# Reading attention heads back from a DRAM scratch: whole 128-row tiles against 20-row transfers over two groups

## Chip, cores, metric

One core of one Trainium2 chip. The metric is the device time of one execution in microseconds (us), lower is better.

## The reference

Two layers, each made of an attention with a compressive memory and a feed-forward block, on 2048 tokens of width 640, with 32 heads of only 20 features. The attention runs over four segments of 512 tokens per layer, one after the other.

```python
B, S, D, H = (1, 2048, 640, 32); N = 4; L = S // N          # Dh = 20
for s in range(N):
    logits = einsum('bhqd,bhkd->bhqk', qs, ks) * scale + mask
    p = softmax(logits); a_dot = einsum('bhqk,bhkd->bhqd', p, vs)
    a_mem = (phi(qs) @ M) / (phi(qs) @ z + 1e-06)
    outs.append(g * a_mem + (1.0 - g) * a_dot)
    M = M + phi(ks).T @ vs;  z = z + phi(ks).sum()
# ... [cut: layer norms before, output projection, residual, then x + relu(LN(x) @ w1) @ w2; all twice]
```

## The kernel before

Instructions are laid out by a list scheduler that runs while the program is built: it has a cost for each operation and fixes the order on every engine.

Queries and keys leave the projections as five chunks of 128 feature rows, without regard to heads (128 is no multiple of 20). The score matmuls of this kernel read the 20 rows of each head at partitions 0, 32, 64 and 96. So each chunk is *spilled* to a DRAM scratch, and each group of four heads is *read back* from there into a `pad` tile. All these transfers, and the transposing transfers, are issued by one in-order queue, that of the sync engine (SP; in the trace it issues all 40 spills, 64 read-backs and 54 transposes).

```python
NPAD = 10
pad = sb("pad", [128, NPAD, 2, L])
scr = nc.dram_tensor("scr", [2, D + 12, 2 * L], dt.bfloat16, kind="Internal").ap()

def spill(a, s):                                   # 5 chunks of a segment
    for c in range(FC):
        # ... [cut: wait for the evacuated chunk]
        tk = yield dma("sp", scr_sem[s % 2][c], 400000, lambda e, c=c: e.dma_start(
            scr[s % 2, 128 * c:128 * c + 128, :], stg[:, c].rearrange("p n t -> p (n t)")), ...)

def fill(a, s):                                    # 8 groups of a segment: the read-backs
    for g in range(G):
        # ... [cut: take a buffer sl, wait for the one or two chunks that hold the rows]
        row = scr[s % 2, 80 * g:80 * g + 1, :]
        tk = yield dma("sp", pad_sem[id(sl)], 400000, lambda e, sl=sl, row=row: e.dma_start(
            sl.ap.rearrange("p n t -> p (n t)"),
            bass.AP(tensor=row.tensor, offset=row.offset,
                    ap=[[DH * 2 * L, 4], [2 * L, 32], [1, 2 * L]])), w + sl.tks, issue=550.0)
```

The source of a read-back has three dimensions, written as [step, count]: 4 heads, 32 rows, 1024 elements. Of every 32 rows 12 are never used, because they belong to the next head; they only fill the partitions up to the next multiple of 32. Two other transfers: `xnT<-xn_tok` transposes a normalized segment so that it can be projected, and `phk<-phs` transposes the key features for the memory update.

The softmax here doesn't subtract the row's maximum and nothing guards it: scores larger than these inputs give would overflow.

Of the kernel before, what the change touches and what calls it, by code (L numbers as in the profile page):

```python
# [5 lines left out]
dt = mybir.dt  # L6
# [4 lines left out]
D = 640  # L11
H = 32
DH = 20
NSEG = 4
L = T // NSEG
DFF = 1728
TT = T // 128
FC = D // 128
G = H // 4
# [5 lines left out]
NFULL = DFF // 128  # L25
# [13 lines left out]
class Prog:  # L39
# [44 lines left out]
    def dma(self, e, fn, sem):  # L84
        self.pos[e] += 1
        self.dcnt[id(sem)] = self.dcnt.get(id(sem), 0) + 16
        tk = (sem, self.dcnt[id(sem)])
        self.ops[e].append(("op", fn, sem, 16))
        self.info[(id(sem), tk[1])] = ("dma%d" % id(sem), tk[1], dict(self.K[e]))
        return tk  # L90
# [217 lines left out]
def bass_interleave_layers__memory_aug_infini_attn__dense_activation_relu__prompt_kernel(  # L308
    nc, A_x, A_wq, A_wk, A_wv, A_wo, A_beta, B_x, B_w1, B_w2, out,
):  # L310
    with contextlib.ExitStack() as es:
        sb = lambda name, shape, dtype=dt.bfloat16: es.enter_context(nc.sbuf_tensor(name, shape, dtype))
        sem_ = lambda name: es.enter_context(nc.semaphore(name))
        P = Prog({e: sem_("clk_" + e) for e in ["act", "dve", "pool", "pe"]})
        S = Sched(P)


        NPAD, NXT, NXN, NPT = 10, 2, 2, 2
        wq_r = sb("wq_r", [128, FC, D])
        wk_r = sb("wk_r", [128, FC, D])  # L320
        wv_r = sb("wv_r", [128, FC, D])
# [14 lines left out]
        xn_tok = sb("xn_tok", [128, NXN, 2 * D])  # L336
        stg = sb("stg", [128, FC, 2, L])
        phs = sb("phs", [128, FC * L])
        pad = sb("pad", [128, NPAD, 2, L])
        rtmp = sb("rtmp", [128, 3, L])  # L340
        phk = sb("phk", [128, FC, NJ, 128])
        v_aug = sb("v_aug", [128, 2, NJ, H, DH + 1])
# [19 lines left out]
        STG = [[Slot(stg[:, c, n], "stg") for c in range(FC)] for n in range(2)]  # L362
        PAD = [Slot(pad[:, k], "pad") for k in range(NPAD)]
        pad_sem = {id(s): sem_("pad%d" % k) for k, s in enumerate(PAD)}
        scr = nc.dram_tensor("scr", [2, D + 12, 2 * L], dt.bfloat16, kind="Internal").ap()
        scr_sem = [[sem_("scr%d_%d" % (n, c)) for c in range(FC)] for n in range(2)]
        RT = [Slot(rtmp[:, k], "rt") for k in range(3)]
        PHK = Slot(phk, "phk")
# [8 lines left out]
        OT = [Slot(oT[:, 2 * FC * k:2 * FC * k + 2 * FC], "oT") for k in range(2)]  # L377
        ot_sem = {id(s): sem_("ot%d" % k) for k, s in enumerate(OT)}
        phk_sem = sem_("phk")
        z_sem = sem_("z")  # L380
        HT = Slot(hT, "hT")


# [47 lines left out]
        def consts():  # L431
            tb = yield dma("act", sem_("d_beta"), 16384, lambda e: e.dma_start(
                beta_bc[:], bass.AP(tensor=A_beta.tensor, offset=A_beta.offset, ap=[[0, 128], [1, H]])))
            t2 = yield pool(400, lambda e: e.memset(
                v_aug[:].rearrange("p b j h e -> p (b j h) e")[:, :, DH:DH + 1], 1.0))
            for b in range(2):
                VA[b].tks = [t2]
            za = yield dve(320, 1, lambda e: e.memset(w1_r[:, :, DFF:DFFP], 0.0))
            zb = yield dve(640, 1, lambda e: e.memset(w2_r[DFF - NFULL * 128:128, NFULL, :], 0.0))
            S.set("z1", tks=[za, zb])  # L440
            zr = DFF - NFULL * 128
            for n in range(2):
                tz = yield dma("act", z_sem, 24576, lambda e, n=n: e.dma_start(
                    scr[n, D:D + 12, :].rearrange("r (k t) -> (r k) t", k=2), w2_r[zr:zr + 24, NFULL, 0:512]), [zb])
            S.set("z2", tks=[tz])
            yield Need("stg", 0, 0, 0)
            te = yield act(32, lambda e: e.activation(gt[:, 0, :], beta_bc[:], ACT.Exp), [tb], psum=False)
            ta = yield dve(32, 1, lambda e: e.tensor_scalar(gt[:, 1, :], gt[:, 0, :], 1.0, None, ALU.add), [te])
            tr = yield dve(256, 1, lambda e: e.reciprocal(gt[:, 1, :], gt[:, 1, :]), [ta])
            tg = yield dve(32, 1, lambda e: e.tensor_tensor(gt[:, 2, :], gt[:, 0, :], gt[:, 1, :], ALU.mult), [tr])  # L450
            to = yield dve(128, 1, lambda e: e.tensor_copy(
                omg[:].rearrange("p g i hh o -> p g i (hh o)"),
                gt[:, 1, :].rearrange("p (g hh) -> p g hh", g=G)[:, :, None, :].to_broadcast([128, G, NJ, 4])), [tr])
            S.set("omg", tks=[to])
            tm = None
            for c in range(FC):
                h0, h1 = CH_H0[c], CH_H1[c]
                mc = maskg[:, CH_OFF[c]:CH_OFF[c + 1]].rearrange("p (h e) -> p h e", e=DH + 1)
                t3 = yield dve(21, 1, lambda e, mc=mc: e.memset(mc[:, :, DH:DH + 1], 1.0))
                t4 = yield dve(147, 1, lambda e, mc=mc, h0=h0, h1=h1: e.tensor_copy(  # L460
                    mc[:, :, 0:DH], gt[:, 2, h0:h1][:, :, None].to_broadcast([128, h1 - h0, DH])), [tg])
                t5 = yield pool(400, lambda e, mc=mc, n=h1 - h0, base=128 * c - DH * h0: e.affine_select(
                    out=mc, in_=mc, compare_op=ALU.is_ge, fill=0.0, base=base,
                    pattern=[[-DH, n], [0, DH + 1]], channel_multiplier=1), [t3, t4])
                tm = yield pool(400, lambda e, mc=mc, n=h1 - h0, base=DH - 1 + DH * h0 - 128 * c: e.affine_select(
                    out=mc, in_=mc, compare_op=ALU.is_ge, fill=0.0, base=base,
                    pattern=[[DH, n], [0, DH + 1]], channel_multiplier=-1), [t5])
            S.set("maskg", tks=[tm])
# [125 lines left out]
        def spill(a, s):  # L594
            for c in range(FC):
                ev = yield Need("stg", a, s, c)
                before = S.events.get(("filled", a, s - 2) if s > 1 else ("filled", a - 1, s + 2), [])
                tk = yield dma("sp", scr_sem[s % 2][c], 400000, lambda e, c=c: e.dma_start(
                    scr[s % 2, 128 * c:128 * c + 128, :], stg[:, c].rearrange("p n t -> p (n t)")),
                    ev + before, issue=350.0)  # L600
                S.set("packed", a, s, c, tks=[tk])

        def fill(a, s):
            got = []
            for g in range(G):
                sl = yield Acq(PAD)
                w = yield Need("z2")
                w = list(w)
                for c in range(80 * g // 128, min(FC - 1, (80 * g + 91) // 128) + 1):
                    t = yield Need("packed", a, s, c)  # L610
                    w += t
                row = scr[s % 2, 80 * g:80 * g + 1, :]
                tk = yield dma("sp", pad_sem[id(sl)], 400000, lambda e, sl=sl, row=row: e.dma_start(
                    sl.ap.rearrange("p n t -> p (n t)"),
                    bass.AP(tensor=row.tensor, offset=row.offset,
                            ap=[[DH * 2 * L, 4], [2 * L, 32], [1, 2 * L]])), w + sl.tks, issue=550.0)
                S.set("pad", a, s, g, tks=[sl, tk])
                got.append(tk)
            S.set("filled", a, s, tks=got)

# [111 lines left out]
        def scores(n):  # L732
            a, r = divmod(n, NSEG * G)
            s, g = divmod(r, G)
            pt = yield Acq(PTS)
            pd = yield Need("pad", a, s, g)
            sl, pd = pd[0], pd[1:]
            mk = []
            for u, js in enumerate(ROUNDS):
                yield Acq([X])  # L740
                yield Acq([Y])
                fns = []
                for z, j in enumerate(js):
                    N = L - 128 * j
                    o = 0 if z == 0 else 512 - N
                    for hh in range(4):
                        fns.append((lambda e, j=j, hh=hh, N=N, o=o: e.matmul(  # L747
                            ps[:, hh, o:o + N], sl.ap[32 * hh:32 * hh + DH, 0, 128 * j:128 * j + 128],
                            sl.ap[32 * hh:32 * hh + DH, 1, 128 * j:L]), z == len(js) - 1 and hh in (1, 3)))
                w = PT_W[u]  # L750
                t0, t1 = yield pe(200.0 + w / 2.4, fns, pd + X.tks + Y.tks)
                ex = []
                for k, (bkp, tk) in enumerate(((X, t0), (Y, t1))):
                    tx = yield act(2 * w, lambda e, k=k, bkp=bkp, u=u, w=w: e.activation(  # L754
                        pt.ap[:, 2 * k:2 * k + 2, PT_AT[u]:PT_AT[u] + w], bkp.ap[:, :, 0:w], ACT.Exp, scale=SCALE),
                        [tk] + pt.tks)
                    bkp.release(tx)
                    ex.append(tx)
                for j in js:
                    reg = pt.ap[:, :, PT_OFF[j]:PT_OFF[j] + 128]  # L760
                    tm = yield pool(600.0, lambda e, reg=reg: e.affine_select(  # L761
                        out=reg, in_=reg, pattern=[[0, 4], [1, 128]], compare_op=ALU.is_ge, fill=0.0, base=0,
                        channel_multiplier=-1), ex)
                    mk.append(tm)
            sl.release(t0, t1)
            S.set("p", n, tks=[pt] + mk)

        def apply(n):
# [171 lines left out]
```

## Time and profile before

| | before |
|---|---|
| median of 3 runs | 689.62 us (688.59 to 693.67) |
| span of the profiled run | 685.0 us |
| tensor engine busy / idle | 597.6 / 87.4 us |
| mean granted tensor clock | 0.948 |
| read-backs | 64 of 256 KB |

The page of the kernel before. First the busy times of the engines (share of the span, instruction counts); then, in 40 equal slices, the busy tenths of the tensor engine and the granted clock; then the chain of waits by engine, which follows the work that ended last backwards.

```profile
PE 597.6 (87%) x6344; PEld 335.3 (49%) x6344; DVE 394.6 (58%) x1191; ACT 422.6 (62%) x586; POOL 179.2 (26%) x284
...
PE   0863953889998999999999999977998799999998
...
PEclk9985885899999999999999999998999999999999
...
PE 67%; DMA 18%; DVE 12%; SPq 1%; ACT 1%; issue 1%
```

The tensor engine bounds the middle and the end. It starves in slices 2 to 7 (counted from 0) and again in 26 and 27, and the clock falls there too.

Busy time by stretch, kernel before. Each row is a stretch in us and its length, then the busy time and instruction count of PE, weight loads, DVE, ACT and POOL, then the granted clock, the mean busy share of the 16 DMA engines, and GB/s. Apart from the first row, which is a look inside the early stage, the cuts are the first score matmul of segments 1, 3, 7 and 8 of the eight.

```profile
core 0: us, PE busy (x) PEld busy (x) DVE busy (x) ACT busy (x) POOL busy (x), PEclk, DMA share, GB/s
40.00:45.00 5.00, 2.37 (x56) 1.39 (x53) 3.98 (x13) 4.62 (x8) 1.41 (x2) 0.98 0.25 97
...
33.00:190.00 157.00, 114.84 (x1313) 61.11 (x1313) 97.61 (x299) 104.40 (x146) 50.41 (x76) 0.82 0.60 135
190.00:448.00 258.00, 252.95 (x2936) 142.46 (x2932) 174.44 (x516) 197.79 (x271) 82.10 (x128) 1.00 0.37 80
448.00:535.00 87.00, 75.05 (x794) 41.56 (x790) 49.77 (x154) 50.95 (x70) 20.62 (x33) 0.94 0.34 72
535.00:685.00 150.00, 141.82 (x1267) 85.08 (x1263) 60.71 (x172) 62.19 (x88) 20.16 (x33) 0.99 0.23 47
```

Between 40 and 45 us the tensor engine works 2.37 us of 5, and the DMA share is 0.25: only four of the sixteen DMA engines work, by time. In that stretch the packet records hold, but for a few of 4 bytes, only 2 KB packets, 44 to 50 a microsecond at 84 ns each.

The sync queue of the kernel before in its early stage: start, length, line and transfer (L598 spills, L613 reads back, L515 transposes).

```profile
31.06 0.32 SPq L598 DMA_DIRECT2D scr<-stg  x1
33.69 0.53 SPq L613 DMA_DIRECT2D pad<-scr  x1
34.98 0.32 SPq L598 DMA_DIRECT2D scr<-stg  x1
39.89 4.27 SPq L613 DMA_DIRECT2D pad<-scr  x4
45.60 7.99 SPq L515 DMA_TRANSPOSE phk<-phs  x1
53.63 7.64 SPq L515 DMA_TRANSPOSE xnT<-xn_tok  x2
```

By the trace's semaphore times, the spills of 31.06 and 34.98 land 8.8 and 8.1 us later; the quickest of the 40 land in 2.0 us (so the one issued at 351.19, with a DMA share of 0.09 in the 2 us before it).

The issues of the two transfers (ns: least, median, most; first and last start):

```profile
L613 SPq DMA_DIRECT2D pad<-scr x64: 509/534/682, 27.2 to 547.3; - x64
L598 SPq DMA_DIRECT2D scr<-stg x40: 314/326/889, 24.0 to 530.8; - x40
```

### The profile page before, as it was taken

How to read it: one execution, taken by the hardware profiler on the slowest of the kernel's cores; microseconds unless marked ns; L12 is line 12 of the kernel's file. 1: busy time of each engine (PE TensorE's matmuls, PEld its weight loads, DVE VectorE, ACT ScalarE, POOL GpSimd, SP SyncE). 2: the span in 40 equal slices, each digit the busy share in tenths (PEclk: the TensorE clock that was granted, in tenths of full speed). 3: DMA queues.
4: the chain of work that ended last, by engine and by line, in shares of the span. 5: the costliest groups of instructions: out<-in, count | busy, mean ns of one | idle time of the engine just before them, and what ended most of it. 6: DMA issues, size and time to landing. Idle time of an engine off the chain costs nothing.

```text
span 685.0 us, 15109 instructions
## 1 busy us (share of the span) xinstructions
PE 597.6 (87%) x6344; PEld 335.3 (49%) x6344; DVE 394.6 (58%) x1191; ACT 422.6 (62%) x586; POOL 179.2 (26%) x284
## 2 busy tenths in 40 slices
PE   0863953889998999999999999977998799999998
PEld 0331431444445654566545654544644465475645
DVE  5181574688648565764687676743964575434102
ACT  0381873688777676866788667953377567804040
POOL 0233341332323332232333332321132223210000
PEclk9985885899999999999999999998999999999999
DMA  5568459542661515280424502564023810050201
GB/s 163 180 119 216 138 181 153 128 119 70 108 131 48 72 38 104 101 131 2 78 110 109 100 2 42 117 114 83 2 46 103 141 38 31 2 106 11 67 11 40
DMA packets 99340, 60.90 MB, mean 89 GB/s; under 512 B 80136, under 2 KB 84664, under 8 KB 99272
## 3 DMA queue, kind: packets, MB, share of 16 engines
q1 hardware_dynamic: 97552, 52.67, 35.6%
q0 software_dynamic: 1504, 7.21, 3.4%
q8 instruction: 50, 0.82, 0.5%
q14 instruction: 18, 0.15, 0.1%
q10 hardware_dynamic: 216, 0.06, 0.0%
HBM read 27.11 MB, written 13.16 MB: 59 GB/s over the span
## 4 chain that ended last, share of the span: by engine, by line
PE 67%; DMA 18%; DVE 12%; SPq 1%; ACT 1%; issue 1%
PE ps L483 43%; PE ps L480 9%; DMA scr<-stg 7%; PE ps L782 7%; PE ps L747 6%; DMA xnT<-xn_tok 4%; DMA oT<-o_sb 3%; DVE stats L491 3%; DMA phk<-phs 1%; DVE xn_tok L533 1%; DMA pad<-scr 1%; PE ps L701 1%; DVE o_sb L671 1%; PE ps L659 1%; DMA x_sb<-in_A_x_dram 1%
## 5 line engine op out<-in xcount | busy, mean ns | idle before, releaser
L754 ACT ACTIVATE PT<-ps 128x1024 bf16<-128x1024 f32 (+1 forms) x384 | 317.4, 880 | 132.4 <-PE ps L747 131.5
L761 POOL TENSOR_SCALAR_AFFINE_SELECT PT<-PT 128x512 bf16<-128x512 bf16 x256 | 165.2, 657 | 390.6 <-ACT PT L754 390.4
L483 PE MATMUL ps<-w_r,hT 128*128 128x320 bf16 x832 | 139.1, 303 | 0.0
L483 PE MATMUL ps<-xnT,w_r 128*128 128x512 bf16 x448 | 126.9, 379 | 0.0
L816 DVE TENSOR_TENSOR x_sb<-x_sb,ps 128x320 bf16<-128x320 bf16 x128 | 61.8, 484 | 107.0 <-PE ps L483 106.4
L483 PEld LDWEIGHTS ps<-w_r,hT 128*128 128x128 bf16 x832 | 79.0, 98 | 32.8 <-issue 4.1
L747 PE MATMUL ps<-pad 20*128 20x512 bf16 (+3 forms) x1024 | 71.8, 313 | 14.0 <-ACT PT L754 12.7
L782 PEld LDWEIGHTS ps<-v_aug,PT 128*128 128x128 bf16 x2560 | 73.7, 96 | 11.3 <-POOL PT L761 2.6
L861 ACT ACTIVATE hT<-ps 128x512 bf16<-128x512 f32 x76 | 45.1, 598 | 53.8 <-PE ps L483 53.0
L782 PE MATMUL ps<-v_aug,PT 128*128 128x21 bf16 x2560 | 74.7, 173 | 0.9 <-DVE stats L491 0.4
L483 PEld LDWEIGHTS ps<-xnT,w_r 128*128 128x128 bf16 x448 | 42.7, 98 | 44.9 <-issue 2.2
L747 PEld LDWEIGHTS ps<-pad 20*128 20x128 bf16 x1024 | 20.7, 92 | 79.5 <-issue 36.0
L491 DVE BATCH_NORM_STATS2 stats<-x_sb 128x6 f32<-128x320 bf16 x128 | 55.2, 465 | 4.4 <-DMA x_sb<-in_A_x_dram 4.4
L483 PE MATMUL ps<-wo_r,oT 128*128 128x320 bf16 x256 | 49.2, 306 | 0.0
L483 PE MATMUL ps<-wv_r,xnT 128*128 128x320 bf16 x256 | 48.8, 306 | 0.0
L480 PE MATMUL ps<-xnT,wk_r 128*128 128x512 bf16 x40 | 16.2, 404 | 36.7 <-DMA xnT<-xn_tok 35.0
L641 ACT ACTIVATE stg<-stg 128x512 bf16<-128x512 bf16 x60 | 38.0, 634 | 15.3 <-DVE rtmp L639 15.2
L483 PE MATMUL ps<-xnT,wq_r 128*128 128x512 bf16 x160 | 46.8, 395 | 0.0
L483 PE MATMUL ps<-xnT,wk_r 128*128 128x512 bf16 x160 | 46.5, 401 | 0.0
L568 ACT ACTIVATE stg<-ps 128x512 bf16<-128x512 f32 x43 | 25.6, 599 | 33.4 <-PE ps L483 32.4
L791 DVE RECIPROCAL rden<-ps 128x16 f32<-128x16 f32 x64 | 16.2, 252 | 50.9 <-PE ps L782 50.7
L480 PE MATMUL ps<-xnT,w_r 128*128 128x512 bf16 x112 | 42.7, 381 | 0.3
(65 smaller groups left out, 573.5 us busy)
## 6 DMA issues: line engine op xcount, KB each, us to landing
pad<-scr SPq DMA_DIRECT2D x64, 256.0 KB
scr<-stg SPq DMA_DIRECT2D x40, 256.0 KB, 3.0
out_dram<-x_sb SPq DMA_DIRECT2D x16, 160.0 KB, 1.8
w_r<-in_B_w_dram POOLq DMA_DIRECT2D x5, 432.0 KB, 6.6
x_sb<-in_A_x_dram POOLq DMA_DIRECT2D x3, 640.0 KB, 6.7
w_r<-in_B_w_dram POOLq DMA_DIRECT2D x2, 640.0 KB, 8.0
wk_r<-in_A_wk_dram SPq DMA_DIRECT2D x1, 800.0 KB, 7.3
wq_r<-in_A_wq_dram SPq DMA_DIRECT2D x1, 800.0 KB, 8.9
```

The lines of the kernel that those rows point to most:

```text
L480: bk, tk = yield pe(mm_ns(n), [(lambda e, bk, a=a, b=b: e.matmul(bk.ap[:, 0:n] if len(b.shape) == 2 else bk.ap[:, 0:n].rearrange("p (i n) ...
L483: tk = yield pe(mm_ns(n), [(lambda e, k=k, a=a, b=b, bk=bk: e.matmul(bk.ap[:, 0:n] if len(b.shape) == 2 else bk.ap[:, 0:n].rearrange("p (i ...
L491: tk = yield dve(320, 1, lambda e, c2=c2: e.bn_stats(stats6[:, t, c2, :], x_sb[:, t, c2 * 320:(c2 + 1) * 320]), xt)
L568: lambda e, sg=sg, bk=bk: e.activation(sg.ap, bk.ap[:, :], ACT.Copy),
L641: te = yield act(512, lambda e, q=q: e.activation(q, q, ACT.Exp), [tr] + p, psum=False)
L747: fns.append((lambda e, j=j, hh=hh, N=N, o=o: e.matmul(ps[:, hh, o:o + N], sl.ap[32 * hh:32 * hh + DH, 0, 128 * j:128 * j + 128], sl.ap[32 ...
L754: tx = yield act(2 * w, lambda e, k=k, bkp=bkp, u=u, w=w: e.activation(pt.ap[:, 2 * k:2 * k + 2, PT_AT[u]:PT_AT[u] + w], bkp.ap[:, :, 0:w] ...
L761: tm = yield pool(600.0, lambda e, reg=reg: e.affine_select(out=reg, in_=reg, pattern=[[0, 4], [1, 128]], compare_op=ALU.is_ge, fill=0.0, ...
L782: fns.append((lambda e, i=i, hh=hh, j=j: e.matmul(od[:, i, hh, :], pt.ap[:, hh, PT_OFF[j] + 128 * (i - j):PT_OFF[j] + 128 * (i - j) + 128] ...
L791: tr = yield dve(96, 1, lambda e: e.reciprocal(rd.ap, od[:, :, :, DH:DH + 1]), [tk] + rd.tks)
L816: ta = yield dve(320, 1, lambda e: e.tensor_tensor(x_sb[:, t, 320 * hf:320 * hf + 320], x_sb[:, t, 320 * hf:320 * hf + 320], bk.ap[:, 0:32 ...
L861: lambda e, dc=dc, bk=bk: e.activation(hT[:, dc, :], bk.ap[:, :], ACT.Relu), [tk] + HT.tks)
```

## The change

Its intent: read only the 20 useful rows of a head, and two groups at a time. 64 reads of 256 KB become 128 reads of 80 KB, and the zero rows behind the scratch are not needed any more.

```diff
-        NPAD, NXT, NXN, NPT = 10, 2, 2, 2
+        NPAD, NXT, NXN, NPT = 5, 2, 2, 2
-        pad = sb("pad", [128, NPAD, 2, L])
+        pad = sb("pad", [128, NPAD, 2, 2, L])
-        scr = nc.dram_tensor("scr", [2, D + 12, 2 * L], ...)
+        scr = nc.dram_tensor("scr", [2, D, 2 * L], ...)
 # ... [cut: the two zero transfers of 24 KB go, and the read-backs' wait for them]
-                tk = yield dma("sp", scr_sem[s % 2][c], 400000, ...          # spill: the scheduler's cost alone
+                tk = yield dma("sp", scr_sem[s % 2][c], 262144, ...
-            for g in range(G):
+            for g in range(0, G, 2):
-                for c in range(80 * g // 128, min(FC - 1, (80 * g + 91) // 128) + 1):
+                for c in range(80 * g // 128, (80 * g + 159) // 128 + 1):
-                row = scr[s % 2, 80 * g:80 * g + 1, :]
-                tk = yield dma("sp", pad_sem[id(sl)], 400000, lambda e, sl=sl, row=row: e.dma_start(
-                    sl.ap.rearrange("p n t -> p (n t)"),
-                    bass.AP(..., ap=[[DH * 2 * L, 4], [2 * L, 32], [1, 2 * L]])), w + sl.tks, issue=550.0)
-                S.set("pad", a, s, g, tks=[sl, tk])
+                for hh in range(4):
+                    src = scr[s % 2, 80 * g:80 * g + 160, :].rearrange("(g h d) t -> d h g t", g=2, d=DH)[:, hh]
+                    tk = yield dma("sp", pad_sem[id(sl)], 81920, lambda e, sl=sl, src=src, hh=hh: e.dma_start(
+                        sl.ap[32 * hh:32 * hh + DH].rearrange("p g n t -> p g (n t)"), src), w + sl.tks, issue=550.0)
+                for z in range(2):
+                    S.set("pad", a, s, g + z, tks=[sl, tk])
 # ... [cut: the scores use sl.ap[:, g % 2] and release the buffer after the second group]
```

More of the change, by code (lines that the diff above doesn't have):

```diff
@@ L364, in bass_interleave_layers__memory_aug_infini_attn__dense_activation_relu__prompt_kernel @@
         pad_sem = {id(s): sem_("pad%d" % k) for k, s in enumerate(PAD)}
-        scr = nc.dram_tensor("scr", [2, D + 12, 2 * L], dt.bfloat16, kind="Internal").ap()
+        scr = nc.dram_tensor("scr", [2, D, 2 * L], dt.bfloat16, kind="Internal").ap()
         scr_sem = [[sem_("scr%d_%d" % (n, c)) for c in range(FC)] for n in range(2)]
@@ L379, in bass_interleave_layers__memory_aug_infini_attn__dense_activation_relu__prompt_kernel @@
         phk_sem = sem_("phk")
-        z_sem = sem_("z")
         HT = Slot(hT, "hT")
@@ L440, in consts @@
             S.set("z1", tks=[za, zb])
-            zr = DFF - NFULL * 128
-            for n in range(2):
-                tz = yield dma("act", z_sem, 24576, lambda e, n=n: e.dma_start(
-                    scr[n, D:D + 12, :].rearrange("r (k t) -> (r k) t", k=2), w2_r[zr:zr + 24, NFULL, 0:512]), [zb])
-            S.set("z2", tks=[tz])
             yield Need("stg", 0, 0, 0)
@@ L597, in spill @@
                 before = S.events.get(("filled", a, s - 2) if s > 1 else ("filled", a - 1, s + 2), [])
-                tk = yield dma("sp", scr_sem[s % 2][c], 400000, lambda e, c=c: e.dma_start(
+                tk = yield dma("sp", scr_sem[s % 2][c], 262144, lambda e, c=c: e.dma_start(
                     scr[s % 2, 128 * c:128 * c + 128, :], stg[:, c].rearrange("p n t -> p (n t)")),
@@ L604, in fill @@
             got = []
-            for g in range(G):
+            for g in range(0, G, 2):
                 sl = yield Acq(PAD)
-                w = yield Need("z2")
-                w = list(w)
-                for c in range(80 * g // 128, min(FC - 1, (80 * g + 91) // 128) + 1):
+                w = []
+                for c in range(80 * g // 128, (80 * g + 159) // 128 + 1):
                     t = yield Need("packed", a, s, c)
                     w += t
-                row = scr[s % 2, 80 * g:80 * g + 1, :]
-                tk = yield dma("sp", pad_sem[id(sl)], 400000, lambda e, sl=sl, row=row: e.dma_start(
-                    sl.ap.rearrange("p n t -> p (n t)"),
-                    bass.AP(tensor=row.tensor, offset=row.offset,
-                            ap=[[DH * 2 * L, 4], [2 * L, 32], [1, 2 * L]])), w + sl.tks, issue=550.0)
-                S.set("pad", a, s, g, tks=[sl, tk])
+                for hh in range(4):
[4 more added lines that the diff above has]
+                    S.set("pad", a, s, g + z, tks=[sl, tk])
                 got.append(tk)
@@ L737, in scores @@
             sl, pd = pd[0], pd[1:]
+            sp = sl.ap[:, g % 2]
             mk = []
@@ L747, in scores @@
                         fns.append((lambda e, j=j, hh=hh, N=N, o=o: e.matmul(
-                            ps[:, hh, o:o + N], sl.ap[32 * hh:32 * hh + DH, 0, 128 * j:128 * j + 128],
-                            sl.ap[32 * hh:32 * hh + DH, 1, 128 * j:L]), z == len(js) - 1 and hh in (1, 3)))
+                            ps[:, hh, o:o + N], sp[32 * hh:32 * hh + DH, 0, 128 * j:128 * j + 128],
+                            sp[32 * hh:32 * hh + DH, 1, 128 * j:L]), z == len(js) - 1 and hh in (1, 3)))
                 w = PT_W[u]
@@ L764, in scores @@
                     mk.append(tm)
-            sl.release(t0, t1)
+            if g % 2:
+                sl.release(t0, t1)
             S.set("p", n, tks=[pt] + mk)
```

## The prediction

> **What bounds the kernel.** The tensor engine: 597.6 us busy of 685.0 (page, busy time). Its 87 us of idleness, from the table of busy time by stretch: about 19 before the first matmul, 40 between 20 and 130 us (70 busy of 110), 7 in 130-230, 8 in 445-470, 7 in 470-560. In 40-70 and 90-130 its granted clock is also down, to 0.58 and 0.70. The chain of waits gives DMA 18%, of which spills to the scratch 7%, layer-norm transposes 4%, output transposes 3%, reads of the scratch 1%.
>
> **What the reads really cost.** They are blamed little, but clog others. A spill (256 KB, same size) posts 16 DMA completions, a read-back only 5. From 40 to 45 us, with only read-backs moving, the DMA share is 0.25 at 97 GB/s: four engines of 16. [...] One 2 KB packet takes 84 ns, so a read-back is 32 x 84 ns = 2.7 us on those engines, a segment's eight 21.5 us. Spills and transposes need all 16 engines and queue behind: spills land in 2.0 us when free, but 8 to 10.7 us at 31, 35, 83, 85, 531; the key-feature transpose issued at 45.6 moves nothing before 52 and lands at 57.2; the next segment's transposes land at 66.1, with the tensor engine idle (9.1 us again at 107-116).
>
> **The change.** 64 reads of 256 KB become 128 of 80 KB: 16.8 to 10.5 MB. [...] A pair of groups occupies an engine 1.3 us instead of 5.4. Cost: the in-order sync queue issues 64 more transfers at about 0.53 us (the old read-back's median), +34 us on 187 us of issuing, 4 us per segment; 16 in a row can hold a transpose back. The first pair waits for two spilled chunks instead of one, some 2 us, hidden under projections. Matmuls, exponentials and masks are unchanged; the static order of all engines shifts.
>
> **On the critical path** (estimates): segment 0 to the second projection (66 us now): -12. Segment 1 to the third (116 now): -12, because spills at 83-85 land 7 us sooner and transposes find empty engines. 120-230: -4. 445-470: -5. 520-550: -4. Half-clock time: -3. Elsewhere 0. Together -40 us.
>
> Predicted: **652 us**, 634 to 674 eight times in ten. Faster by over 2%: 0.92; within: 0.07; slower: 0.01.
>
> **Right if:** read-backs post 10 or 11 completions; the stretch of 0.25 share is gone; spills land in about 2 us, worst under 6; the second projection starts near 54 us, the third near 92; tensor-engine busy about 590, its idleness about 60; read-back issues stay 0.5-0.6 us.
>
> **Wrong if:** read-backs still use few engines or packets run far over 84 ns; issue takes 1 us or more, making the sync queue the limit in the first two segments; the vector engine (8.6 us busy of 10 at 100-110 us) already limits there; release by pairs stalls reads, with transposes queued after them; or the new static order opens holes of 10-20 us in the middle.

The 1.3 us for a pair of groups, 4 reads of 4 packets of 84 ns, rests on ten engines, which was then the expectation.

## More of the kernel before

The transpose issued at 45.60 moves about 400 of its 256-byte packets between 46 and 48 us, none from 48 to 52, and lands at 57.2.

What the tensor engine waited for over the whole of the kernel before: total us, times, longest.

```profile
PE ps L480 <- DMA xnT<-xn_tok: 35.0, 4, 18.9
...
PE ps L480 <- DMA oT<-o_sb: 8.2, 4, 4.9
PE ps L701 <- DMA phk<-phs: 6.5, 1, 6.5
...
PE ps L747 <- DMA pad<-scr: 1.2, 1, 1.2
```

The tensor engine hardly waits for the read-backs (1.2 us). The transposes are waited for.

The sync queue waits too, before a read-back, for the spill that it reads, and whatever stands behind that read-back in the queue waits with it. Total us, times, longest:

```profile
SPq L613 <- DMA scr<-stg: 62.8, 23, 8.5
```

## The result, and the profile after

| | before | after |
|---|---|---|
| median of 4 runs of the same rounds | 690.94 us | 643.05 us |
| ratio | | 0.9302 (0.9261 to 0.9342) |
| span of the profiled run | 685.0 us | 639.8 us |
| tensor engine busy / idle | 597.6 / 87.4 | 585.0 / 54.7 us |
| mean granted clock | 0.948 | 0.976 |

A ratio is the mean time of one kernel's fast runs over the mean of the other's fast runs of the same rounds, so it is not quite the ratio of the medians. The brackets are a 95% interval.

The page after:

```profile
PE 585.0 (91%) x6344; PEld 332.2 (52%) x6344; DVE 403.1 (63%) x1200; ACT 418.1 (65%) x577; POOL 178.1 (28%) x284
...
PE   0857948899999999999999999999999999999998
...
PEclk9987968999999999999999999999999999999999
...
PE 78%; DVE 15%; DMA 4%; ACT 2%; issue 1%; SPq 0%; POOL 0%
```

DMA falls from 18% to 4% of the chain. The late hole is gone; the early one is shorter but still there.

Stretches after, cut at the same score matmuls; again the first row looks inside the early stage:

```profile
core 0: us, PE busy (x) PEld busy (x) DVE busy (x) ACT busy (x) POOL busy (x), PEclk, DMA share, GB/s
28.00:34.00 6.00, 6.00 (x38) 3.15 (x36) 2.97 (x8) 4.75 (x8) 0.46 (x2) 1.00 0.71 211
...
33.00:168.00 135.00, 107.47 (x1292) 58.49 (x1292) 99.24 (x300) 100.46 (x141) 48.74 (x76) 0.89 0.56 138
168.00:424.00 256.00, 254.41 (x2954) 143.75 (x2954) 180.17 (x529) 199.43 (x274) 81.87 (x128) 1.00 0.31 72
424.00:488.00 64.00, 62.70 (x738) 35.08 (x736) 44.73 (x134) 46.65 (x62) 21.04 (x33) 1.00 0.32 64
488.00:640.00 152.00, 146.30 (x1303) 88.54 (x1303) 65.32 (x183) 62.78 (x89) 20.57 (x33) 1.00 0.23 48
```

Put the two tables side by side. The first stage goes from 157 to 135 us (idleness 42.2 to 27.5, busy 114.8 to 107.5 with the clock at 0.89 instead of 0.82). The middle, 258 and 256, hardly changes. The stage before the last segment goes from 87 to 64. So the 45 us come from two places, about 22 us each. (Some feed-forward matmuls moved from this stage into the tail, 794 to 738 and 1267 to 1303, so the last two stages are best taken together: 237 to 216 us, idleness 20.1 to 7.0, busy 216.9 to 209.0.)

The sync queue after (L592 spills, L607 reads back, L509 transposes):

```profile
31.24 1.16 SPq L592 DMA_DIRECT2D scr<-stg  x2
34.89 3.82 SPq L607 DMA_DIRECT2D pad<-scr  x8
40.83 3.11 SPq L509 DMA_TRANSPOSE phk<-phs  x1
47.40 5.86 SPq L509 DMA_TRANSPOSE xnT<-xn_tok  x2
```

The same two spills land 3.6 and 3.9 us after issue instead of 8.8 and 8.1. The issue of the key-feature transpose takes 3.11 us instead of 7.99. It still lands 10.7 us after its issue (11.6 before); its gain is mostly that it is issued 4.8 us earlier. Over the kernel the median spill takes 2.4 us to land instead of 3.0, and the worst 7.3 instead of 10.7. The sync queue's waits for spills shrink from 62.8 us to:

```profile
SPq L607 <- DMA scr<-stg: 23.0, 13, 3.5
```

What the tensor engine waits for after:

```profile
PE ps L474 <- DMA xnT<-xn_tok: 19.9, 2, 18.8
PE ps L741 <- ACT PT L748: 12.9, 14, 2.0
PE ps L694 <- DMA phk<-phs: 4.7, 1, 4.7
```

18.8 us of the first line are the start of the kernel, in both. The waits for output transposes fall from 8.2 to 1.5 us in total.

The issues after. 128 reads at 336 ns are 43 us of the sync queue; the old 64 at 534 ns were 34 (by the medians; summed over the traces 45.7 and 34.2).

```profile
L607 SPq DMA_DIRECT2D pad<-scr x128: 274/336/1460, 28.1 to 495.3; - x128
L592 SPq DMA_DIRECT2D scr<-stg x40: 319/343/641, 23.3 to 491.3; - x40
```

### The profile page after: what moved, and what is told of

It is laid out like the page before. It is cut to its first block, busy times and chain, and to the rows that moved or that the text cites. A ratio compares the mean times of both kernels' runs of the same rounds, so it can differ in the third digit from the quotient of the medians.

```text
span 639.8 us, 15133 instructions
## 1 busy us (share of the span) xinstructions
PE 585.0 (91%) x6344; PEld 332.2 (52%) x6344; DVE 403.1 (63%) x1200; ACT 418.1 (65%) x577; POOL 178.1 (28%) x284
## 2 busy tenths in 40 slices
DMA packets 97220, 54.57 MB, mean 85 GB/s; under 512 B 81136, under 2 KB 85616, under 8 KB 97152
## 3 DMA queue, kind: packets, MB, share of 16 engines
q1 hardware_dynamic: 95504, 46.38, 31.8%
## 4 chain that ended last, share of the span: by engine, by line
PE 78%; DVE 15%; DMA 4%; ACT 2%; issue 1%; SPq 0%; POOL 0%
PE ps L477 49%; PE ps L474 11%; PE ps L777 8%; PE ps L741 7%; DVE stats L485 3%; DVE xn_tok L527 2%; DMA xnT<-xn_tok 2%; ACT PT L748 1%; DMA scr<-stg 1%; DVE x_sb L811 1%; PE ps L694 1%; PE ps L652 1%; DVE o_sb L664 1%; DVE hT L854 1%; DMA x_sb<-in_A_x_dram 1%
## 5 line engine op out<-in xcount | busy, mean ns | idle before, releaser
L477 PE MATMUL ps<-w_r,hT 128*128 128x320 bf16 x832 | 135.1, 299 | 0.0
L741 PE MATMUL ps<-pad 20*128 20x512 bf16 (+3 forms) x1024 | 70.5, 308 | 13.1 <-ACT PT L748 12.9
L856 ACT ACTIVATE hT<-ps 128x512 bf16<-128x512 f32 x63 | 37.7, 598 | 54.9 <-PE ps L477 53.8
L741 PEld LDWEIGHTS ps<-pad 20*128 20x128 bf16 x1024 | 20.6, 92 | 76.7 <-ACT PT L748 34.2
L477 PE MATMUL ps<-wo_r,oT 128*128 128x320 bf16 x256 | 48.1, 299 | 0.0
L562 ACT ACTIVATE stg<-ps 128x512 bf16<-128x512 f32 x46 | 27.4, 599 | 31.1 <-PE ps L477 30.3
L477 PE MATMUL ps<-xnT,wk_r 128*128 128x512 bf16 x160 | 46.5, 392 | 0.0
L477 PE MATMUL ps<-xnT,wq_r 128*128 128x512 bf16 x160 | 44.0, 382 | 0.0
L854 DVE TENSOR_SCALAR hT<-ps 128x512 bf16<-128x512 f32 x49 | 33.5, 683 | 11.0 <-PE ps L477 10.8
```

What stands on the lines that cost most here:

```text
L477: tk = yield pe(mm_ns(n), [(lambda e, k=k, a=a, b=b, bk=bk: e.matmul(bk.ap[:, 0:n] if len(b.shape) == 2 else bk.ap[:, 0:n].rearrange("p (i ...
L562: lambda e, sg=sg, bk=bk: e.activation(sg.ap, bk.ap[:, :], ACT.Copy),
L741: fns.append((lambda e, j=j, hh=hh, N=N, o=o: e.matmul(ps[:, hh, o:o + N], sp[32 * hh:32 * hh + DH, 0, 128 * j:128 * j + 128], sp[32 * hh: ...
L854: th = yield evac(512, 1, lambda e, dc=dc, bk=bk: e.tensor_scalar(hT[:, dc, :], bk.ap[:, :], 0.0, None, ALU.max), lambda e, dc=dc, bk=bk: ...
L856: lambda e, dc=dc, bk=bk: e.activation(hT[:, dc, :], bk.ap[:, :], ACT.Relu), [tk] + HT.tks)
```

## The experiments

Three theories stood after the result. **E**: the old reads kept four DMA engines so busy that spills and transposes, which use all sixteen (16 semaphore updates each), queued behind them. **B**: fewer bytes (the sync queue's total went from 52.67 to 46.38 MB). **O**: the scheduler, given other costs and buffers, found a better static order; the orders on all engines do differ from before to after.

To keep order out of it, the experiments change only what the issuing function of a read does; the scheduler sees the same costs. The static orders on the tensor, vector and POOL engines were compared and are identical to the kernel each was made from (in a_whole the scalar queue also issues the two zero transfers again). Names with b_ have the order of before, those with a_ that of after, except a_late, a_quad and a_pre, which are rescheduled (a_late came out with the order of after on all engines but POOL).

"Work on an engine" below is reads per segment x packets per engine x the median time of a packet, an estimate from the packet records: 21.5 us before, 5.4 after, with 2 KB packets of 84 ns. (The reads of a_k4 and a_k2, whose rows are neighbours, went as half as many packets of 4 KB and 159 ns; their expectations still reckon with 84 ns for each 2 KB.) The number of engines is counted in every trace. The semaphore of a transfer gets 5 updates per read before, 11 after, 16 per spill. Before, with 5, four packets are under way at once and the DMA share is 0.25; after, with 11, nine or ten of the 2 KB packets are under way at 77% of the moments sampled between 37 and 38 us. So the updates are read here as one more than the engines where they are fewer than 16, and 16 as sixteen engines. The packets under 512 bytes bear it out: between kernels of one order they differ by just one for each engine of a read. They are 80136 in before (64 reads on 4), 80904 in b_rows20_k4 (256 on 4), 82440 in b_rows20 (256 on 10) and 83976 in b_rows32 (256 on 16); and 81136 in after (128 on 10), 80368 in a_k4 (128 on 4), 80112 in a_k2 (128 on 2) and 82416 in a_256 (256 on 10).

### Series 1: order, engines, bytes

**a_whole**: order of after, old reads.

```diff
-  scr[...].rearrange("(g h d) t -> d h g t", g=2, d=DH)[:, hh]  ->  sl.ap[32 * hh:32 * hh + DH]     # hh = 0..3
+  ap=[[DH * 2 * L, 4], [2 * L, 32], [1, 2 * L]] of group g + hh  ->  sl.ap[:, hh]                   # hh = 0, 1 only
```

> The changed kernel's static order on every engine, with the old read-backs (64 of 256 KB, four engines each). Three theories: E (engines: the old reads block four engines that spills and transposes need), B (bytes: 16.8 MB became 10.5 MB), O (order: the scheduler's new static order made the gain). E and B: the gain goes, 680 to 700 us. O: the gain stays, 640 to 650 us.

Measured: 707.93 us, ratio 1.0295 (1.0218 to 1.0372). The gain is not only gone: with the old reads the new order is 3% slower than the old one. O falls. That it would be this bad was not foreseen.

**a_k4**: order, bytes and issues of after, but four engines.

```diff
-  src = scr[...].rearrange("(g h d) t -> d h g t", g=2, d=DH)[:, hh]        # 20 rows outermost
+  src = bass.AP(..., ap=[[40 * 2 * L, 4], [2 * L, 10], [1, 2 * L]])         # 4 outermost, wrong rows on purpose
```

> The changed kernel with the same order, the same 128 issues and the same bytes, but each read described so that it runs on four engines (its rows come from the wrong places, so the output is wrong on purpose). Work on each of these engines per segment: 16 x 10 packets x 84 ns = 13.4 us, against 5.4 in the changed kernel and 21.5 in the old one. E: between the two kernels, 655 to 670 us. B and O: as the changed kernel, 640 to 648 us.

Measured: 669.61 us, 0.9754 (0.9691 to 0.9818); 5 updates per read. More than half of the gain is lost with order and bytes unchanged; B alone expected 640 to 648. The issue also went from 336 to 600 ns, though, 34 us in all, so this run by itself leaves a part to the sync queue (at the price that b_issue shows below, some 16 of the 30 us, an estimate):

```profile
L609 SPq DMA_DIRECT2D pad<-scr x128: 599/600/1197, 27.9 to 522.3; - x128
```

(It passed the comparison although its queries and keys are wrong. The comparison evidently does not see the attention well behind the residual; passing it proves nothing for the wrong-row kernels.)

**b_rows20**: order of before, each read as four reads of 20 rows on ten engines.

```diff
-  e.dma_start(sl.ap[...], bass.AP(..., ap=[[DH * 2 * L, 4], [2 * L, 32], [1, 2 * L]]))
+  for hh in range(4):
+      e.dma_start(sl.ap[32 * hh:32 * hh + 20], scr[s % 2, 80 * g + DH * hh:80 * g + DH * hh + 20, :])
```

> The old kernel's static order on every engine, each read-back replaced by four reads of 20 rows (10 engines, 160 KB a group, 256 issues instead of 64; at 0.34 us that is 86 us of issuing instead of 34). E: most of the gain, 645 to 662 us. B: 645 to 662 us as well. O: no gain, 685 to 700 us.

Measured: 646.49 us, 0.9428 (0.9374 to 0.9483), 11 updates per read. Five sixths of the gain (5.7 of 6.8 per cent) without touching the order of anything.

**b_rows32**: the same with 32 rows, so that all the old bytes are read, on 16 engines.

> As b_rows20, but four reads of 32 rows: 16 engines, all the old 256 KB a group, the old order, 256 issues. Work on each engine is as in b_rows20 (8 packets a group). E: as b_rows20 within 1%. B: no gain, 685 to 700 us. O: no gain.

Measured: 657.73 us, 0.9582 (0.9510 to 0.9653), 16 updates per read. With all the bytes still read, it gains four per cent, so B alone falls here. It is 1.6% behind b_rows20, more than the 1% that E allowed. Bytes are one possible cause. The other is the issue, 422 ns against 331, over 256 reads 23 us.

### Series 2: the price of an issue

**after_again**: the yardstick.

> The changed kernel itself, as the yardstick of this series on this chip: ratio 0.93 to its own kernel before.

Measured: 642.19 us, 0.9327 (0.9273 to 0.9380).

**b_issue**: the kernel before, three tiny reads ahead of each read-back.

```diff
+  for z in range(3):
+      e.dma_start(tinyrd[:, k, z, :], scr[s % 2, 80 * g:80 * g + 32, 16 * z:16 * z + 8])     # 32 rows of 16 bytes
   e.dma_start(sl.ap[...], bass.AP(..., ap=[[DH * 2 * L, 4], [2 * L, 32], [1, 2 * L]]))
```

> The old kernel, its old read-backs and its order, with three tiny reads (32 rows of 16 bytes, 16 engines) issued ahead of each read-back: 256 issues on the sync queue instead of 64, almost no bytes. My prediction counted 64 more issues as a cost that could hold transposes back. If issuing costs: 192 more at about 0.33 us are 63 us of the sync queue, and the time rises by 10 us or more. If only occupied engines matter: within 1% of the kernel before.

Measured: 727.27 us, 1.0552 (1.0488 to 1.0617). My theory that only occupied engines count falls. The sync queue is in order, and an issue is time on it:

```profile
L621 SPq DMA_DIRECT2D tinyrd<-scr x192: 302/421/1518, 26.5 to 584.9; - x192
```

192 x 421 ns are 81 us of issuing for 38 us of time. (The 192 tiny reads add 9216 packets under 512 bytes, 89352 against 80136: 32 and 16 each, by the count above 32 rows and sixteen engines. The tiny packets themselves are little work, 6144 of 7 ns. But the spills land later too, 5.3 us at the median against 3.0, which this run does not explain; the 38 us are the price of the extra reads as a whole.) But it makes b_rows32 a much better witness: both have 256 issues (115 us in b_issue, 108 in b_rows32), nearly the same bytes and the same order. Only the engines of the read-backs differ, 4 or 16, and the ratios are 1.0552 and 0.9582.

**b_rows20_k4**: b_rows20 on four engines (a source that begins with a 4, wrong rows).

> As b_rows20 (old order, 256 reads of 40 KB, 160 KB a group), but each read described so that it runs on four engines (rows from the wrong places, on purpose). Work on each of the four per segment 13.4 us, against 21.5 in the old kernel and 5.4 in b_rows20. E: ratio 0.965 to 0.99, well above the 0.943 of b_rows20. B: as b_rows20. The issues may take 0.6 us each instead of 0.33, as they did in a_k4; b_issue tells what that is worth.

Measured: 675.94 us, 0.9825 (0.9770 to 0.9879), in the range of E, with 256 issues of 600 ns. Against b_rows20 the bytes, order and count of reads are the same; engines and issue time differ. At b_issue's price the 69 us more of issuing could be the whole difference of 27 us, so by itself this run does not separate the two.

**a_late**: later loads.

```diff
-  w = yield Need("filled", 0, 0)     # third segment's input, output weights
+  w = yield Need("stg", 0, 1, 0)
-  w = yield Need("o", k)             # feed-forward weights, a piece per group
+  w = yield Need("o", k + 3)
```

> The changed kernel with the loads of the third segment's input and of the output and feed-forward weights moved later (input and output weights when the second segment's first projection is evacuated, each feed-forward piece three groups later), so that they do not share the engines with the transposes issued at 41 to 49 us, which took 7 to 11 us to land. If these loads are what is left of the early wait: 2 to 8 us less than the changed kernel. If the vector engine is the limit there: the same within 2 us.

Measured: 646.79 us, 0.9397 (0.9351 to 0.9443): 4.6 us slower than after_again in the same rounds, a miss. The early part did what was meant: the key-feature transpose lands 4.9 us after issue (10.7 in after), and the second projection starts at 54.2 us instead of 56.9. By the fourth projection it is 164.3 against 159.0. The moved weight pieces now land at 121 to 141 us, beside the transposes issued at 134 and 137 us, which take 6.4 and 5.3 us (3.4 and 3.6 in after). That the whole loss is this was not tested.

### Series 3: the dose, the order, and two attempts to beat it

**a_k2**: as a_k4, two engines (`ap=[[80 * 2 * L, 2], [2 * L, 20], [1, 2 * L]]`).

> As a_k4 (order, issues and bytes of the changed kernel, rows from the wrong places), but each read on two engines: 26.9 us of work on each of them per segment against 13.4 in a_k4 and 21.5 in a_whole. Its issues should take about as long as those of a_k4 (0.6 us), so the step from a_k4 to a_k2 is the engines alone. E: ratio 1.03 to 1.10, above a_whole. B and O: as a_k4, 0.975.

Measured: 734.71 us, 1.0643 (1.0575 to 1.0711), 3 updates per read.

```profile
L609 SPq DMA_DIRECT2D pad<-scr x128: 584/585/1002, 28.4 to 586.7; - x128
```

The issue is as long as in a_k4, even a little shorter; order, bytes and count are the same. Halving the engines alone costs 9%. This is the cleanest of the pairs. It also shows where the loss sits. The median spill takes 5.4 us to land, against 2.9 in a_k4, and the sync queue waits for spills twice as long (a_k4, then a_k2):

```profile
SPq L609 <- DMA scr<-stg: 36.1, 13, 5.0
SPq L609 <- DMA scr<-stg: 78.9, 13, 13.0
```

That the reads themselves arrive later is no rival: the tensor engine's waits for them grow only from 2.3 to 7.4 us, of some 60 us lost.

**a_256**: order of after, each read split into its two groups, 256 issues.

```diff
-  e.dma_start(sl.ap[32 * hh:32 * hh + DH].rearrange("p g n t -> p g (n t)"), src)
+  for z in range(2):
+      e.dma_start(sl.ap[32 * hh:32 * hh + DH, z], scr[s % 2, 80 * (g + z) + DH * hh:80 * (g + z) + DH * hh + DH, :])
```

> The changed kernel's order, engines and bytes, but each read of two groups split into two of 20 rows by 2 KB: 256 issues instead of 128, some 43 us more on the sync queue. Against the changed kernel (0.930 and 0.933 to the kernel before) it gives the price of issues: if they matter as b_issue said, plus 5 to 15 us; if not, within 2 us. Against b_rows20 (0.943, the same reads in the old order) it gives the order alone.

Measured: 649.30 us, 0.9404 (0.9346 to 0.9462). 42 us more of issuing cost about 6 us (the interval of a_256 overlaps that of after_again, 0.9273 to 0.9380, and just misses that of after). Against b_rows20 (0.9428), which has the same reads in the old order, it is the same within the intervals: with spread reads the order is worth nothing that I can see.

**a_quad**: four groups per read.

```diff
-  NPAD = 5;  pad = sb("pad", [128, NPAD, 2, 2, L]);  for g in range(0, G, 2)
+  NPAD = 2;  pad = sb("pad", [128, NPAD, 4, 2, L]);  for g in range(0, G, 4)
```

> Reads of four groups at once: 64 issues of 160 KB on ten engines, two buffers of four groups instead of five of two. Issues cost 22 us instead of 43, but the first read of a segment waits for three spilled chunks and buffers come free half a segment at a time. If issuing is the price, up to 5 us less than the changed kernel; if coarseness is, 5 to 20 us more.

Measured: 654.11 us, 0.9476 (0.9418 to 0.9534). Half the issues, 11 us slower: coarseness costs more than the issues save. The first scores start at 38.6 us instead of 32.6.

**a_pre**: early statistics.

```diff
+  def early_stats():                         # its own stream: bn_stats and rstd of segments 1 to 3, layer 1
+      for s in range(1, NSEG):
+          w = yield Need("x%d" % s)
+          ...
+          S.set("ln", s, tks=[tch])
```

> The changed kernel with the layer-norm statistics of the first layer's segments 1 to 3 taken as soon as their input has landed, in a stream of their own, instead of after the projections of the segment before. The chain of waits of the changed kernel has the vector engine at 15%, statistics at 3%: the second and third projections (56.9 and 96.9 us) wait for them. Expected 628 to 638 us, against 642 to 643 of the changed kernel; if the tensor engine's order or the transposes limit there instead, the same within 2 us.

Measured: 661.23 us, 0.9577 (0.9508 to 0.9646): 18 us slower than after, a miss. The first transpose of the second segment does land early, at 42.9 us. But the key-feature transpose, issued at 41.6, now takes 15.9 us to land, and the tensor engine, in order, waits 8.4 us for it; the second projection starts at 59.1, later than in after. The larger loss comes between the fourth and the fifth projection (160.4 to 253.3 us, against 159.0 to 234.5); I did not find its cause. Neither attempt beats the changed kernel.

### All together

| kernel | order | engines per read | reads x issue | work on an engine per segment | ratio to before |
|---|---|---|---|---|---|
| before | old | 4 | 64 x 0.53 us | 21.5 us | 1 |
| b_issue | old | 4 | 64 x 0.53, 192 tiny x 0.42 | 21.5 | 1.0552 |
| b_rows20_k4 | old | 4 | 256 x 0.60 | 13.4 | 0.9825 |
| b_rows32 | old | 16 | 256 x 0.42 | 5.4 | 0.9582 |
| b_rows20 | old | 10 | 256 x 0.33 | 5.4 | 0.9428 |
| a_k2 | new | 2 | 128 x 0.59 | 25.4 | 1.0643 |
| a_whole | new | 4 | 64 x 0.53 | 21.5 | 1.0295 |
| a_k4 | new | 4 | 128 x 0.60 | 12.7 | 0.9754 |
| a_256 | new | 10 | 256 x 0.33 | 5.4 | 0.9404 |
| after | new | 10 | 128 x 0.34 | 5.4 | 0.9302, 0.9327 |

In the new order the time follows the work on an engine, and not the issuing: a_whole has the least issuing of the five (34 us) and is the second slowest.

## Why the prediction was right or wrong

**Mechanism: right.** The old source begins with a count of 4, and its reads ran on four engines (5 updates, a share of 0.25). Ten for the new reads was an expectation until the result showed it (11 updates). In the forms tried here the engines were 4 where the source begins with a 4 (before, a_whole, a_k4, b_rows20_k4), 2 where it begins with a 2 (a_k2), 10 for 20 rows (after, b_rows20), and 16 for 32 rows (b_rows32) and for the spills' 128. Three changes of engines at constant order and bytes move the time as they should: a_k4 to a_k2 (+9%), b_issue to b_rows32 (-9%, at equal issuing), after to a_k4 (+5%, with longer issues).

**"64 more transfers at about 0.53 us, +34 us": wrong in size.** A read on ten engines takes 0.336 us to issue, so the read-backs' issuing rose by 9 us only (11.5 summed over the traces); the sync queue's total even fell, from 187 to 164 us, as the issues of the transposes took 96 us in all instead of 130. But the worry itself was sound: b_issue and a_256 show that an issue has a price, about half of the issuing time in the kernel before (38 of 81 us), about a seventh in the changed one (6 of 42).

**"Segment 0: -12, segment 1: -12, 120-230: -4": near.** The second projection starts at 56.9 us instead of 66.2 (-9.3), the third at 96.9 instead of 116.3 (-19.4 in all), and the scores of the fourth segment start 23.5 us earlier. The sum of 28 was too high. In the chain of waits after, the layer norm on the vector engine, a limit that the prediction named among its risks, fills 39.7 to 48.1 us, and only then is the last transpose issued. But a_pre, with earlier statistics, did not start the second projection sooner (59.1), while a_late, with later weight loads, started it at 54.2, the full 12 us ahead. So what the first term had wrong was at least in part that the transposes would find their engines empty: loads stood there (with them moved, in a_late, the key-feature transpose landed 4.9 us after its issue instead of 10.7).

**"445-470: -5; 520-550: -4; half-clock time: -3": too small.** These are the terms that missed. The lead stays at 23 to 24 us from the fourth segment's scores to the seventh's, and is 46.9 at the eighth's. The idleness of this late stage and the tail fell by 13 us and their busy time by 8. Over the whole kernel busy time fell by 12.6 us for the same 6344 matmuls, where 3 were forecast (though the sign "busy about 590" given in advance meant 8). The same 512-wide matmul of the key projection took 401 ns on the mean before and 392 after, that of the query projection 395 and 382. In the traces of before and after the granted clock is 1.00 or 0.50, and each stretch at 0.50, but for a rest after the last matmul, lasts one to eight times 3.41 us (3.41 to 27.31). The engine need not be idle for it: before, the clock falls to 0.50 at 44.8 us, after 3.4 us that held 1.56 us of tensor work, and stays there until 72.1, through the waits of 6.5 and 6.0 us that follow. The nine falls of the two traces, the last matmul's aside, came after 3.4 us with 0.1 to 1.8 us of work, though three other such stretches, with 1.7 to 2.0, kept the full clock. In all, 72 us ran at half clock before and 31 after, with 38.0 and 15.5 us of tensor work in them. The 512-wide query and key projection matmul of before took 634 ns there (16 of them, median) and 379 at full clock; by that 0.4 of such work is the slow clock, 9.0 of the 12.6 us (an estimate). By the granted 0.50 it is half, 11.3 us (an estimate too), and the other traces bear the half out: busy time less half of that at half clock is 576 to 579 us in all fourteen (578.6 before, 577.3 after), while the busy time itself runs from 585 to 611. So here a wait is paid twice, in idleness and in slow matmuls after it.

**The total.** Forecast -40 as idleness 37 and clock 3; measured -45 in the profiled runs, as idleness 32.7 and busy 12.6. 652 was forecast, 643 measured, within the range of 634 to 674. That the total came so near is partly luck: the idleness was forecast 4 us too high and the clock's share some 6 to 8 us too low, and within the idleness the early terms were too large and the late ones too small.

**Signs given in advance.** 11 updates, the quarter-share stretch gone, busy near 590 (585.0), idleness near 60 (54.7), the second projection near 54 and the third near 92 (56.9 and 96.9): near or as said. "Worst spill under 6 us" failed: 7.3 us at 107.5, behind output transposes issued at 104 and beside two weight loads.

**Bytes stay open in part.** They are at most the 1.6% between b_rows32 and b_rows20, of which the 23 us less issuing may be a part. No run reads fewer bytes with all else equal.

## What to carry to other kernels

Count the engines of a transfer (its semaphore's updates, or the DMA share while it runs alone), and not only its bytes: the source here whose outermost count is 4 made a 256 KB read occupy four engines (5 updates, a share of 0.25) for 2.7 us (estimate, 32 packets of 84 ns). A transfer that nobody waits for can still be what everyone waits for, if it stands in front of the others on the same engines: the tensor engine waited 1.2 us for the read-backs, and spreading the same bytes over sixteen engines took 4.2% off the time (b_rows32). Look at transfers whose time to landing is several times its least (spills of 10.7 us against 2.0). When the tensor engine is short of work, price a wait at its length plus the slow clock behind it (72 us at half clock before, 31 after).

Price the issues too: 192 more of them, 81 us of issuing, came with 38 us more time (b_issue). Medians on the sync queue here: 0.33 to 0.34 us for 20-row reads on 10 engines (331 ns for 40 KB in b_rows20, 336 for 80 KB in after, 341 for 160 KB in a_quad), 0.33 to 0.34 for the 128-row spills on 16 (before, after), 0.42 for 32 rows on 16 (b_rows32), 0.53 for 128 rows on 4 (before), 0.59 to 0.60 for 20 rows on 4 or 2 (a_k4, a_k2).
